# Ten of twelve down products by Strassen's scheme, in a recurrent layer followed by an MLP

## The chip, the cores and the metric

The kernel runs on one core of a Trainium2 chip. The metric is the time of one execution on the device in microseconds. A core has five engines that work from queues of their own, each in order: TensorE (PE in the profile, its weight loads PEld), VectorE (DVE), ScalarE (ACT), GpSimd (POOL) and SyncE (SP), which here issues the DMAs.

## The reference

Everything is float32. A recurrent block with a state of 40 x 40 for each of 4 x 8 heads runs over 768 steps; its output, 3072 tokens of 320 numbers, goes through a two-layer MLP.

```python
# r, k, v, w, a, b: (4, 8, 768, 40)
for t in range(S):
    y[:, :, t] = einsum('bhd,bhde->bhe', rt, state)
    Sa = einsum('bhde,bhe->bhd', state, at)
    state = state * wt[:, :, None, :] - einsum('bhd,bhe->bhde', Sa, bt)
    state = state + einsum('bhd,bhe->bhde', vt, kt)
x = y.transpose(0, 2, 1, 3).reshape(3072, 320)
h = x @ w_in                              # w_in: 320 x 2048
g = h * (1.0 / (1.0 + exp(-1.702 * h)))
return g @ w_out                          # w_out: 2048 x 320
```

## The kernel before, in words

The sequence is cut into 12 chunks of 64 steps. A *unit* i = 2c + p is chunk c for one pair p of the four batches, so there are 24 units. For each unit the kernel forms decays (`decay`), scores (`prep`), inverts a triangular matrix in five levels (`inverse`, PSUM tile `ps_level`, SBUF tiles W, E, ES, EX, T), and solves and updates the state (`solve`, tiles A, B, M, zr). The result x of a unit is written to DRAM and read back transposed as `xT` (`part_with`, `get_back`). When both units of a chunk are there, `mlp(c)` handles its 256 tokens.

All matmuls go through `mm` (line 300 of the profile) as 64 x 64 quarters of the array: `QUARTERS` walks over two halves r of the contraction and two halves of the output, so four matmuls of one step use four quarters. One such float32 matmul appears as two records in the profile.

`mlp(c)` has four steps q of the up product (`up`, tile `ps_up`, 256 columns, the tokens), each followed by an activation on ACT (`gelu`), which writes the tile g of q: 512 of the 2048 hidden numbers for the 256 tokens. The down product (`down(p)`, tile `ps_down`) takes 128 tokens at a time: eight parts m of two f of four quarters, 320 columns each, over the whole contraction. Then one engine copies one half of the PSUM pair to `ob`, VectorE adds the other, and SP stores `ob` with two DMAs. Four buffers of g are in turn.

The order of the work is written out by hand in the string `ORDER`: each entry names a task by its number, its engine by a letter (p, a, d, g, s for PE, ACT, DVE, POOL, SP) and the PSUM pair of the four that it uses. `Plan.add` registers a task with the engines that may do it and what it reads and writes; `Plan.listed` gives every task the engine and pair of its entry, and the tasks are issued in that order. So every engine's queue is the subsequence of the string with its letter. The costs that stand beside the tasks (`pe`, `dve`, `act`, `any2`) are not read when the kernel is built.

The weights come as 64-bit pieces (`weight`, raw data in the tile `extra` and in places that are free for the moment) and are made into float32 by ACT, VectorE and POOL in the first part of the run. `w_out_sb` holds w_out as 16 blocks f of 320 columns.

Of the kernel before, what the change touches and what calls it, by code (L numbers as in the profile page):

```python
# [58 lines left out]
class Plan:  # L59
# [29 lines left out]
    def listed(self, text):  # L89

        assert len(text.split()) == len(self.tasks)
        table, out, done = "exp", [], set()
        for one in text.split():
            e = next(e for e in ENGINES if ENGINES[e] in one)
            n, bank = one.split(ENGINES[e])
            t = self.tasks[int(n)]
            assert e in t.engines and t.after <= done and (e == "SP" or (t.pair is None) == (not bank))
            t.engine, t.bank = e, int(bank or 0)
            if e == "ACT" and t.table:
# [8 lines left out]
0s 8s 26s 5s 7s 9s 3a 6s 87p0 88p1 24s 89a1 1s 2s 12s 102a 95d 100p2 90a0 93d 158a 101d2 98p3 96g 10s 94d 17s 97g 16s 99d3  # L108
103p1 4a 11s 132p0 104a1 105d1 142p2 143p3 133a0 106d 130p1 14s 144a3 13s 107p0 15s 18s 151g 108a0 109d0 51s 131a1 110p3 27s
149g 150d 111a3 112d3 159p0 156p1 145a2 161d0 160a0 152g 113p3 345s 92a 162d 25s 153d 114a3 163p2 42s 115d3 34s 19a 274s 264p0  # L110
165d2 265p3 164a2 22d 266a3 166p2 20d 273s 21d 33s 43s 167a2 154p3 168d2 23g 35s 28a 157d1 116p2 155d3 169p1 117a2 118d2 267a0
279d 63s 280g 119p3 277s 171d1 36s 44s 123a3 120d3 343s 125d3 121a 278g 124d3 29d 287a 126p2 170a1 288p0 127a2 30d 172p1 479s
122a3 31d 289a0 128p2 54s 173a1 45s 129d2 32g 62s 174d1 134p3 37a 290d0 175p2 344s 135d3 180a2 146s 178a2 275s 176d2 136p1
179a2 38d 181a2 39d 177a 282g 276s 291d 91s 138a1 182p0 188p3 281d 183a0 186p2 139d 137a1 283p0 187a2 184p1 189a3 40d 140s
292p2 46a 60s 284d0 41g 285p3 185d1 148a 286d3 190p0 293a2 294d2 334p1 335p3 357a 191d0 141s 268g 147s 336a3 315d 192p2 47d
337a1 348d 316p0 194a2 346s 295p3 349d 61s 317a0 195g 347s 358p1 296a3 297d3 360d1 318a0 298p3 271a 361d 319p0 338g 300d3 196s
193a2 320a0 355p2 385d 270s 48d 299a3 362p0 356d2 351g 301p3 363a0 364d0 350g 386p2 197s 302d3 365p0 387a2 269s 352g 359a1
303d3 388a2 323p1 367d0 366a0 321p3 49d 324a1 304p2 322a3 478s 325d1 50g 353p0 309a2 470p3 354d0 209p1 307a2 210p1 310a2 305d2
211p1 308a2 272d 198p0 341a 199p0 72s 212p1 70s 64a 200p0 340s 368p2 52s 342d 339s 69s 201p0 369a2 202p0 370d2 203p0 471a
213p1 65d 214p1 389p2 66d 472a3 483g 204p0 390a2 560s 371p3 67d 306a 53s 215p1 71s 482s 216p1 372a3 217p1 476a 220p2 373d3 68g  # L120
218p1 221p2 477d 219a1 205p0 222p2 206p0 223p2 224p2 78s 559s 207p0 55a 311p3 225p2 79s 312d3 80s 226p2 208a0 58d 313p1 374p3
314d1 227p2 56d 379a3 228p2 229p2 57d 326p0 230a2 59g 393p1 327d0 378a3 391p2 394a1 375d3 231p0 558s 392d2 376a 232p0 233p0
395d1 81s 73a 234p0 480s 381p2 235p0 474s 328p1 475s 382a2 74d 377a3 485d 380a3 236p0 75d 481s 492a 242p2 486d 243p2 82a 76d
484d 77g 383p3 237p0 384d3 244p2 329d1 330d1 488p3 473d 238p0 531d 245p2 487g 246p2 489d3 85d 532p1 708s 239p0 533a1 396p3
331d 534a1 240p0 247p2 397d3 332s 241a0 562s 535p1 83d 490p3 536a1 84d 398p0 706s 572a 491d3 86g 550p1 253p3 399d0 551a 555s
400d0 561s 333s 254p3 401d 255p3 552a1 564d 493p0 402s 556a 567g 570p1 554s 494d0 248p2 705s 563d 566g 249p2 495d0 498d 256p3
571d1 565g 403s 250a2 496a0 251d2 696p1 497g 557d 539p0 252s 537p2 257p3 538a2 704s 540d0 701s 258p3 553d 611d 697a 499d 573p2
259p3 576a2 574d2 784s 710d 700s 260p3 787s 541d0 575d2 404p0 578d 261a3 577g 405p0 579d 698a1 568p2 711g 500p1 406p0 569d2
501a1 407p0 262d3 580p2 702a 502d1 263s 408p0 582d2 409p0 503d 410p0 583d 504a 612p3 411p0 584g 613d3 412p0 614d3 413p0 505p1
709d 414a0 426p3 506d1 427p3 428p3 507d1 429p3 699d 581d2 430p3 615p1 703d 431p3 616a1 785s 585p0 432p3 508d 586a0 433p3 587d0  # L130
434p3 509a 588d 435p3 589d 448p2 436a3 510p1 590p0 511a1 449p2 592d0 591a0 512d1 415p3 513d 416p3 593d 514a 417p3 594g 418p3
515p0 419p3 516a0 517d0 595p1 518d 420p3 596a1 597d1 421p3 598d 422p3 519a 599d 423p3 424p3 520p0 425a3 437p1 521d0 438p1
523d0 522g 439p1 524d0 440p1 525d0 441p1 442p1 526d0 527p3 718p0 528a3 443p1 719d0 929s 444p1 720d0 529p3 445p1 721d0 446p1
530d3 600p0 723d 447a1 542p3 722d 724g 603d0 605a0 619p1 604d0 543d3 450p2 620a1 606d0 544p3 621d1 601d0 602d 617p1 707s 546d3
451p2 618a1 783s 712d 547g 713d 607p0 725p1 608a0 452p2 609p0 453p2 548s 610d0 932s 454p2 727d1 726d1 622p0 728d 545d3 729a
775p1 455p2 623d0 780s 776a 549s 756d 730p3 624p0 456d2 457d2 731d3 458s 459p2 777a1 778g 732d3 786s 788g 781a 779s 626d0
460p2 625d0 627g 733d 795p1 835d 734a 461p2 735p3 791g 462p2 628s 736a3 796d1 737d3 716p0 792g 738d 463p2 782d 739g 1011s
920p1 757p3 925s 464p2 717d0 758a3 629s 759a3 790d 465p2 740p0 789d 466p2 741a0 742d0 921a 797p3 467d2 760p0 1008s 468d2 800a3
923d 652p2 469s 761d0 922a1 653p2 926a 930s 798d3 714p1 799d3 654p2 924s 802d 801g 655p2 934d 803a 656p2 836p0 657p2 715d1
658p2 659p2 837d0 762p3 838d0 927d 660p2 763a3 661p2 764p1 662a2 743d 630p0 744d 928s 631p0 632p0 765d1 804p3 766d1 633p0  # L140
805a3 806d3 634p0 807d 635p0 808a 745p2 636p0 748d2 637p0 749d2 839p1 933g 750d2 638p0 840a1 1009s 751d2 639p0 809p3 746d2
935g 640a0 641p1 810d3 642p1 793p2 747a 811d3 674p0 812d 794d2 813a 752p3 643p1 753a3 814p2 644p1 815a2 816d2 754p3 645p1
755d3 646p1 817d 647p1 818a 767p2 841p3 768d2 648p1 842a3 649p1 819p2 650p1 820a2 821d2 769p3 822d 651a1 823d 675p0 771d3 931s
770d3 772g 824p2 936d 676p0 827a2 828a2 942p1 829a2 677p0 1153s 830a2 937d 945a1 773s 663p3 825d2 664p3 943d1 1156s 826a 665p3
944d1 999p2 947d 946g 666p3 1000a 1004s 980d 940p1 948g 667p3 941d1 668p3 774s 669p3 670p3 831p1 671p3 1001a2 1002d 1003s
832d1 672p3 1005a 1013d 678p0 673a3 1006d 833p2 843p1 679p0 834d2 1007s 844d1 938p2 845d1 680p0 939d2 846p3 681p0 847d3 949p1
1012g 682d0 848p2 950a1 683d0 1014d 684s 685p3 849d2 1015g 1010s 850d2 1021p0 1016g 951d1 686p3 1024a0 1232s 851d 1235s 981p2
687p3 982a2 952d 852s 1022d0 983a2 953g 1144p1 1023d0 688p3 1026d 1145a 1149s 1025d 1027g 984p2 1059d 689p3 1154s 954p0 853s
985a2 1147g 690p3 1158d 1148s 955a0 956d0 986p2 1146a1 957d 1150a 691p3 958d 987a2 1151d 988p0 692p3 989a0 1152s 990d0 959p1
693a3 865p2 960a1 694d3 866p2 961d1 867p2 695s 962d 868p2 963d 1028p0 869p2 1029a0 1030d0 870p2 1031d 1157g 871p2 1159d 1032a  # L150
1060p3 872p2 873p2 1061a3 874p2 1062d3 1033p1 875a2 854p0 1035d1 855p0 1036d 856p0 1037d 1063p3 857p0 1064d3 1034a1 858p0
964p2 859p0 965a2 966d2 1038p1 967d 860p0 1039a1 1040d1 861p0 1041d 1017p3 968a 1042g 862p0 1018d3 863p0 969p2 864a0 876p1
970d2 877p1 972d2 971g 1043p3 973d2 878p1 1044a3 974d2 879p1 975d2 880p1 881p1 1045d3 1019p0 1046d 976p2 1047a 882p1 1020d0
1233s 883p1 977a2 1166p3 884p1 1169a3 1167d3 1377s 978p0 885p1 1168d3 898p2 1171d 1170g 886a1 979d0 887p3 1172a 1048p0 991p1
1051a0 888p3 1052a0 992d1 889p3 1053a0 890p3 1054a0 891p3 1049d0 993p1 1050a 1067p0 994d1 1160g 1155s 892p3 1161d 1068a0 893p3
894p3 1069d0 1380s 895p3 1204d 1065p0 995d1 896p3 996d 1066a0 1231s 1055p1 899p2 897a3 1056d1 997s 1173p0 1223p3 900p2 1174a0
# [92 lines left out]
def rwkv7_gelu_quick(ctx: ExitStack, tc: tile.TileContext, time_d, v_d, w_d, wc_d, ak_d, b_d, rv_d, w_in, w_out, out):  # L249
    nc = tc.nc  # L250
    H, D, S = 8, 40, out.shape[0] // 4
    DM = H * D
    C = 64
    MID = C // 2
    NU = time_d.shape[0]
    PIECE = w_in.shape[2]
    NF = w_in.shape[0] * PIECE // DM
# [717 lines left out]
    def mlp(c):  # L975
# [47 lines left out]
        for p in BITS:  # L1023
            down(p)
# [8 lines left out]
    for i in range(NU):  # L1033
# [10 lines left out]
        if i % 2:  # L1044
            mlp(i // 2)
# [84 lines left out]
```

## Time and profile before

| | |
|---|---|
| median of three runs | 679.92 us (675.03 to 681.91) |
| profiled execution | 682.79 us |
| its span, first to last instruction | 681.1 us |
| granted TensorE clock, mean | 0.990 |
| PE busy | 652.0 us, 96% of the span |
| DVE, ACT, POOL busy | 445.5, 330.7, 176.7 us |
| busy time of the group ps_up | 254.4 us, 3840 records |
| busy time of the group ps_down | 240.3 us, 3072 records |
| the chain that ended last | PE 91%, DMA 4% |

In a group's line of the profile come the source line, engine and operation, the tiles, the shapes, the number of records, then busy time and the mean length of one. Records of matmuls overlap each other: the 3072 of ps_down last 430 ns each on the mean, but one starts every 70 ns or so. In the slices the span is cut into 40 parts of 17 us, with the busy share of each in tenths. The timeline merges neighbouring instructions of one kind into one line: start, length from the first start to the last end, and how many.

### The profile page before, as it was taken

Reading aid. Unit: us, or ns where it says so; the run is one execution under the profiler, and the core shown is the slowest. Engines: PE = TensorE matmul, PEld = TensorE weight load, DVE = VectorE, ACT = ScalarE, POOL = GpSimd, SP = SyncE. Lnnn points to the kernel's source line nnn. Section 1 sums busy time; section 2 is a strip of 40 time slices with the busy share of each in tenths; the row PEclk is TensorE's granted clock in tenths of the full one; section 3 lists DMA queues with packets and bytes.
Section 4 is the critical chain, followed back from the end, with each engine's and each line's share of the span. In section 5 each row is a group of like instructions: output and inputs, shape, how many; then the busy total and the mean of one; then the engine's idle time right before and its main releaser. Section 6 shows DMA issues by size and latency. Waiting matters only on the chain.

```text
span 681.1 us, 42181 instructions
## 1 busy us (share of the span) xinstructions
PE 652.0 (96%) x19488; PEld 572.4 (84%) x19488; DVE 445.5 (65%) x906; ACT 330.7 (49%) x688; POOL 176.7 (26%) x204
## 2 busy tenths in 40 slices
PE   5777999999999999999999999999999999999997
PEld 5667888997987788888888898899899799889996
DVE  4687877777867668767776587868556766675001
ACT  4675845544564654664545445455454354252110
POOL 5443444225123123123123211321412421300000
PEclk9788999999999999999999999999999999999999
DMA  7874755205314314432404413513502312200100
GB/s 235 275 244 148 228 158 173 89 14 155 108 50 139 103 45 125 124 108 67 121 23 131 140 34 107 154 33 106 149 29 71 121 51 58 58 13 23 51 12 21
DMA packets 35312, 69.73 MB, mean 102 GB/s; under 512 B 5440, under 2 KB 14656, under 8 KB 35136
## 3 DMA queue, kind: packets, MB, share of 16 engines
q1 hardware_dynamic: 35136, 67.03, 32.8%
q8 instruction: 153, 2.51, 1.6%
q14 instruction: 23, 0.19, 0.1%
HBM read 59.15 MB, written 7.86 MB: 98 GB/s over the span
## 4 chain that ended last, share of the span: by engine, by line
PE 91%; DMA 4%; ACT 1%; DVE 1%; issue 1%; SPq 0%; ACTq 0%; DVEq 0%
PE ps_up L300 31%; PE ps_down L300 30%; PE ps_level L300 9%; PE ps_y L300 5%; PE ps_B L300 4%; PE ps_X L300 2%; PE ps_N L300 2%; PE ps_rz L300 2%; PE ps_RV L300 2%; PE ps_A L300 1%; DMA ak<-in_ak 1%; PE ps_zT L300 1%; PE ps_Q L300 1%; DMA time<-in_time 1%; PE ps_T L300 1%
## 5 line engine op out<-in xcount | busy, mean ns | idle before, releaser
L300 PE MATMUL ps_up<-xT_all,w_sb 64*64 64x256 f32 x3840 | 254.4, 377 | 2.0 <-DMA xT_all<-x_dram 1.1
L300 PE MATMUL ps_down<-w_sb,g 64*64 64x320 f32 x3072 | 240.3, 430 | 1.1 <-issue 0.9
L300 PEld LDWEIGHTS ps_up<-xT_all,w_sb 64*64 64x64 f32 x3840 | 172.9, 133 | 17.7 <-issue 2.5
L300 PEld LDWEIGHTS ps_down<-w_sb,g 64*64 64x64 f32 x3072 | 143.3, 133 | 31.4 <-issue 1.6
L988 ACT ACTIVATE g<-ps_up 128x1024 f32<-128x1024 f32 x48 | 49.1, 1024 | 44.7 <-PE ps_up L300 44.3
L709 POOL TENSOR_TENSOR EX<-ES,quads 128x512 f32<-128x512 f32 x29 | 38.3, 1323 | 115.5 <-DVE ES L702 83.1
L751 ACT COPY W<-ps_level 128x512 f32<-128x512 f32 x56 | 32.7, 585 | 69.1 <-PE ps_level L300 67.4
L300 PEld LDWEIGHTS ps_level<-W,EX 64*64 64x64 f32 x2560 | 59.2, 134 | 5.8 <-DVE T L830 0.2
L300 PE MATMUL ps_level<-W,EX 64*64 64x64 f32 (+1 forms) x2560 | 56.2, 217 | 0.0
L753 DVE TENSOR_TENSOR E<-two,ps_level 128x256 f32<-128x256 f32 x80 | 33.1, 415 | 34.7 <-ACT W L751 30.7
L707 ACT ACTIVATE EX<-ES,quads 128x256 f32<-128x256 f32 x80 | 36.3, 501 | 30.4 <-DVE ES L702 29.9
L619 POOL TENSOR_TENSOR ak<-ak,FT 128x512 f32<-128x512 f32 x16 | 22.0, 1378 | 76.2 <-DMA ak<-in_ak 54.4
L300 PE MATMUL ps_level<-PT,EX 64*64 64x64 f32 (+2 forms) x1280 | 34.9, 244 | 5.7 <-DVE EX L723 4.8
L300 PEld LDWEIGHTS ps_level<-PT,EX 64*64 64x64 f32 x1280 | 32.6, 145 | 8.9 <-DVE EX L723 5.7
L702 DVE STREAM_TRANSPOSE ES<-E 128x256 f32<-128x256 f32 x80 | 35.2, 442 | 4.7 <-DVE E L753 0.5
L300 PE MATMUL ps_y<-M,bh 64*64 64x104 f32 (+1 forms) x768 | 34.8, 247 | 1.3 <-DVE M L907 0.8
L300 PE MATMUL ps_y<-RV,kh 64*64 64x104 f32 (+1 forms) x768 | 34.9, 247 | 0.3 <-DVE EX L723 0.3
L891 ACT COPY B<-ps_B 128x416 f32<-128x416 f32 (+1 forms) x34 | 16.5, 492 | 33.5 <-PE ps_B L300 33.2
L300 PEld LDWEIGHTS ps_y<-RV,kh 64*64 64x64 f32 x768 | 28.9, 133 | 2.0 <-DVE M L907 0.5
L907 DVE TENSOR_TENSOR M<-ps_X,later 128x832 f32<-128x832 f32 (+1 forms) x24 | 23.8, 993 | 9.8 <-PE ps_X L300 9.5
L627 POOL TENSOR_TENSOR kh<-time,G 128x320 f32<-128x320 f32 x18 | 16.2, 902 | 48.4 <-PE ps_y L300 34.4
L300 PEld LDWEIGHTS ps_y<-M,bh 64*64 64x64 f32 x768 | 27.0, 133 | 1.9 <-DVE M L907 1.2
(131 smaller groups left out, 1097.2 us busy)
## 6 DMA issues: line engine op xcount, KB each, us to landing
ak<-in_ak SPq DMA_DIRECT2D x48, 160.0 KB
rv<-in_rv SPq DMA_DIRECT2D x48, 160.0 KB
time<-in_time SPq DMA_DIRECT2D x24, 320.0 KB
xT_all<-x_dram SPq DMA_DIRECT2D x48, 160.0 KB
wc<-in_wc SPq DMA_DIRECT2D x20, 264.0 KB
logw<-in_w SPq DMA_DIRECT2D x24, 160.0 KB
RV<-in_v SPq DMA_DIRECT2D x24, 160.0 KB
b<-in_b SPq DMA_DIRECT2D x48, 80.0 KB
```

The source lines that it names most:

```text
L300: nc.tensor.matmul(o, lhsT, rhs, start=start, stop=True, skip_group_check=True)
L619: plan.add(R, {"DVE": 690.0, "POOL": 1270.0, "sbuf": True}, lambda t: of(t.engine).tensor_mul(ahT(), ahT(), FT_of(i)), reads=T("ak", "FT") ...
L627: plan.add(R + 4, {"POOL": 870.0, "DVE": 490.0, "sbuf": True}, lambda t, n=n, dst=dst: of(t.engine).tensor_mul(dst(i)[:, :, :D], by_head(t ...
L702: plan.add(rank, dve(256), lambda t: nc.vector.transpose(ES(n), source(t)), writes=[key("ES", n, 6)], **reads)
L707: nc.scalar.activation(dst[:, :, h], ES(n), ACT.Copy, scale=quads[:, h, :1])
L709: of(t.engine).tensor_mul(dst, ES(n).unsqueeze(2).to_broadcast([128, 8, 2, 32]), quads.unsqueeze(1).to_broadcast([128, 8, 2, 32]))
L751: plan.add(rank, any2(512), lambda t: copy(t.engine)(tiles_of(W(n + 1)), blocks(psum(t, ""), 64)), writes=[key("W", n + 1, 5)], pair=pair)
L753: plan.add(rank, dve(256), lambda t: nc.vector.tensor_sub(tiles_of(E(n + 1)), every(two32, [128, 2, 4, 32]), blocks(psum(t, ""), 64)[:, :, ...
L891: plan.add(R, any2(4 * wide), lambda t: copy(t.engine)(dst(), some(psum(t, "")[:, :, :208])), writes=[("Bv", i)] if x and c > 0 else T("B" ...
L907: plan.add(R + 1, dve(8 * wide), lambda t: nc.vector.tensor_tensor(M_of(i)[:, :, :wide].rearrange("p (j b) n -> p b j n", b=2), some(psum( ...
L988: plan.add(-45, {"ACT": 1030.0, "table": "gelu"}, lambda t: nc.scalar.activation(g_of(c * NQ + q).rearrange("p m r n -> p r m n"), psum(t, ...
```

## The change

For chunks 2 to 11 (`FAST`) the down product is computed by Strassen's scheme (in the form with seven products and fifteen additions). The 256 tokens are split into two halves p, the contraction of 2048 into two halves s, the 320 output columns into two halves d of 160. Seven products of 128 x 1024 by 1024 x 160 take the place of eight. The four differences of blocks of w_out that the scheme needs, T1 to T4, are formed once (`factors`) in `extra`, after the weights are ready. For each fast chunk, four combinations of blocks of g (S1 to S4) are formed, three of them in place in g, each in two parts j; the products go to three PSUM pairs (`ps_fast`, with two, three and two products); and their sums form the four blocks of the output in `of_fast`, with `new6` and `new7` between. The last chunk computes the product M2 last, and stores in three steps, the last of them half on ACT's queue.

The layout of g changes for all chunks, so that one half of the tokens is contiguous; there are six buffers of g and not four. The string `ORDER` is new as a whole, 2840 entries in place of 2700. A scratch area that the program reserves is set to 2048 bytes; no DMA here is issued by POOL. The other two chunks keep the old form of the down product.

```diff
+    FAST = range(2, 12)
...
-                     ... xT=3, g=4, ob=1), 4)
+                     ... xT=3, g=6, ob=1, S10=1, S11=1, of=1, n6=1, n7=1), 4)
...
-    g_of = lambda n: buf("g", n, [128, 2, 2, 256])
+    g_of = lambda n: buf("g", n, [128, 2, 4, 128])
+    DH = DM // 2
+    S1 = single("S1", [128, 2, 4, 128])
+    T1, T2, T3, T4 = (extra[:, k * PIECE:(k + 1) * PIECE].rearrange("p (j f n) -> p j f n", j=2, f=4) for k in range(4))
+    B11, B12, B21, B22 = (w_out_sb.rearrange("p (j s f d n)": ...)[:, :, s, :, d] for s in BITS for d in BITS)
+    of_fast, new6, new7 = (single(name, [128, n, DH]) for name, n in (("of_fast", 4), ("new6", 3), ("new7", 2)))
+
+    def factors():
+        for dst, a, b, ... in ((T1, B12, B11), (T2, B22, T1), (T3, B22, B12), (T4, B21, T2)):
+            for j in BITS:
+                ... of(t.engine).tensor_sub(dst[:, j], a[:, j], b[:, j])
+
+    def fast_down(c):
+        last = c == NU // 2 - 1
+        def mixed(j, name, dst, a, b, reads, writes, add=False):      # POOL or DVE, 128x512
+            ... (of(t.engine).tensor_add if add else of(t.engine).tensor_sub)(dst(j), a(j), b(j))
+        def product_of(pair, n, at, a, b, j, reads, first=True):
+            def go(t):
+                po = psum(t, "ps_fast")
+                for f in range(4):
+                    for r, h in QUARTERS:
+                        mm(po[HALF[h], r, at * DH:(at + 1) * DH], a(j)[HALF[r], 2 * (f % 2) + f // 2, h * 64:h * 64 + 64], b[HALF[r], j, f],
+                           first and at == 0 and j == 0 and f == 0)
+        def summed(pair, n, dst, key, name, free=()):                 # ACT or DVE copies, DVE adds
+            ... copy(t.engine)(flat(), psum(t, "")[:, 0, :n * DH])
+            ... nc.vector.tensor_add(flat(), flat(), psum(t, "")[:, 1, :n * DH])
+        def added(dst, a, b, n, reads, uses, name):                   # POOL or DVE, n * 160 columns
+            ... of(t.engine).tensor_add(dst(), a(), b())
+
+        for j in BITS:
+            mixed(j, "A", s1, A21, A22, ..., add=True)                # S1
+            mixed(j, "S3", A21, A11, A21, ...)
+        if last:
+            products(0, *((1, 0, M1, j) for j in BITS))
+        else:
+            products(0, *((n, n % 2, M, j) for j in BITS for n, M in ((2, M2), (1, M1))))
+        S4 = s1 if last else A12
+        for j in BITS:
+            mixed(j, "S2", A11, s1, A11, ...)
+            if not last:
+                mixed(j, "S4", S4, A12, A11, ...)
+        if not last:
+            summed(0, 2, lambda: of_fast[:, :2], "of", "M21")
+            added(of_fast[:, 0], of_fast[:, 0], of_fast[:, 1], 1, ..., "C11")
+        else:
+            summed(0, 1, lambda: of_fast[:, 1:2], "of", "M21")
+        products(1, *((4, 0, M4, j) for j in BITS), *((5, 1, M5, j) for j in BITS), *((6, 2, M6, j) for j in BITS))
+        if last:
+            for j in BITS:
+                mixed(j, "S4", S4, A12, A11, ...)
+        summed(1, 3, lambda: new6, "n6", "M456")
+        added(new6[:, 2], new6[:, 2], of_fast[:, 1], 1, ..., "U")
+        added(new6[:, :2], new6[:, :2], new6[:, 2] broadcast, 2, ..., "XW")
+        products(2, *((n, at, M, j) for j in BITS for n, at, M in ((7, 0, M7), (3, 1, M3))))
+        summed(2, 2, lambda: new7, "n7", "M73")
+        added(of_fast[:, 1], new6[:, 1], new7[:, 1], 1, ..., "C12")
+        added(of_fast[:, 2:], new6[:, :2], new7[:, 0] broadcast, 2, ..., "C2")
+        if last:
+            store(0, ["C12"], slice(1, 2))
+            store(1, ["C2"])
+            ... M2 in pair 0, summed into of_fast[:, 0:1] ...
+            store(0, ["C11"], slice(0, 1))                            # second DMA on ACT's queue
+        else:
+            store(0, ["C11", "C12"])
+            store(1, ["C2"])
...
-        for p in BITS:
-            down(p)
+        if c in FAST:
+            fast_down(c)
+        else:
+            for p in BITS:
+                down(p)
...
+            if i // 2 == min(FAST):
+                factors()
             mlp(i // 2)
...
-    nc = bacc.Bacc("TRN2", target_bir_lowering=False, num_devices=1)
+    nc = bacc.Bacc("TRN2", target_bir_lowering=False, num_devices=1, dynamic_dma_scratch_size=2048)
```

In the fast products, M1 is A11 by B11, M2 is A12 by B21, M3 is S4 by B22, M4 is A22 by T4, M5 is S1 by T1, M6 is S2 by T2 and M7 is S3 by T3, where A are blocks of g and B blocks of w_out.

More of the change, by code (lines that the diff above doesn't have):

```diff
@@ L98, in listed @@
             t.engine, t.bank = e, int(bank or 0)
+            if e == "SP":
+                t.window = t.bank
             if e == "ACT" and t.table:
@@ L245 @@
+2607d 2806d 2609s 2815p1 2810d 2816p1 2819d 2817p1 2820d 2818p1 2811d0 2825p3 2821d1 2822d1 2826p3 2812d0 2823d 2827p3 2824d
+2828p3 2835p0 2829d3 2830d3 2836p0 2831d 2832d 2833s 2834s 2837d0 2838d0 2839s
 """
```

340 lines of the change are left out of this document (198 added, 142 removed).

## The prediction

> **What bounds the kernel now.** I read the page first: its engine table and its slices.
>
> ```profile
> span 681.1 us, 42181 instructions
> ...
> PE 652.0 (96%) x19488; PEld 572.4 (84%) x19488; DVE 445.5 (65%) x906; ACT 330.7 (49%) x688; POOL 176.7 (26%) x204
> ...
> PE   5777999999999999999999999999999999999997
> ...
> DVE  4687877777867668767776587868556766675001
> ...
> PEclk9788999999999999999999999999999999999999
> ```
>
> From the fifth slice (68 us) on TensorE is full, at a full granted clock; VectorE comes next with some seven tenths. The part that is not full is the opening. The sums by stretch say the same in microseconds (columns: length, then busy time of PE, weight loads, DVE, ACT, POOL, then granted clock, DMA share, GB/s):
>
> ```profile
> 0.00:100.00 100.00, 77.76 (x2478) 69.45 (x2482) 70.37 (x109) 62.68 (x148) 46.04 (x66) 0.93 0.70 216
> ...
> 300.00:400.00 100.00, 100.00 (x3062) 85.85 (x3054) 71.66 (x154) 50.38 (x90) 24.63 (x28) 1.00 0.34 96
> ```
>
> 22 us of the 29 us that PE is idle lie in the first 100 us. The waits of TensorE name only small ones: 4.8 us for EX, 3.8 us for the first logw, 1.1 us once for x coming back by DMA. So outside the opening a matmul taken out of the order shortens the span by its own streaming time, as long as what feeds it keeps up.
>
> Busy means are no price here, since spans of neighbouring groups overlap. The timeline of a full stretch gives prices by the distance between starts:
>
> ```profile
> 413.88 0.49 PE L300 MATMUL ps_cum<-logw,edges 64*64 64x160 f32 x6
> 414.16 1.28 PE L300 MATMUL ps_down<-w_sb,g 64*64 64x320 f32 x16
> ...
> 417.01 0.57 PE L300 MATMUL ps_B<-RV,A 64*64 64x104 f32 x16
> 417.37 0.57 PE L300 MATMUL ps_B<-zr,ak 40*64 40x104 f32 x16
> 417.73 1.28 PE L300 MATMUL ps_down<-w_sb,g 64*64 64x320 f32 x16
> 418.81 0.67 PE L300 MATMUL ps_A<-ak 40*64 40x64 f32 x32
> ```
>
> From 417.73 to 418.81 sixteen matmuls of 320 columns start and give way: 67.5 ns each. From 417.37 to 417.73 sixteen of 104 columns: 22.5 ns. The end of the chain agrees and adds the third point:
>
> ```profile
> 657.91 4.32 PE ps_up L300 x80
> 662.23 14.02 PE ps_down L300 x208
> ```
>
> 14.02 us / 208 = 67.4 ns at 320 columns, 4.32 us / 80 = 54.0 ns at 256. Through 22.5, 54.0 and 67.4 runs nearly one straight line of 0.21 ns a column with less than 1 ns beside it.
>
> **TensorE's part.** The group of the down product has 3072 matmul records, 256 for each of 12 chunks. Ten chunks lose theirs: 2560 x 67.4 ns = 172.5 us go. Each of the ten gets seven products of two halves j, four f and four quarters, two records each: 7 x 64 = 448 records of 160 columns, 4480 in all. No long run of 160 columns is in the trace. Between 104 and 256 columns the line gives 22.5 + 56 x 0.207 = 34.1 ns; the lower end is half of 67.4, 33.7 ns; the upper is the short ps_cum burst, whose eight records lie between 413.84 and 414.16, 40 ns each, with the last ps_zT among them. I take 34.1, from the long runs. 4480 x 34.1 ns = 152.8 us come, so **-19.7 us** (-21.5 at 33.7; +6.7 at 40).
>
> [...]
>
> **What feeds it.** Each fast chunk needs eight additions of 128x512 out of SBUF, three reads of PSUM in two steps, and five additions of their sums. By the written order VectorE gets 49 of the 512-wide ones and POOL 31. Nearest rows for VectorE, 128x512: 699 ns (EX by quads), 740 ns (ak by GT), 924 ns (ak by FT). I take 0.72 us: 49 x 0.72 = 35.3 us. Reads of PSUM on VectorE, 45: from the rows at 320 columns (483 and 489 ns) and estimates of 0.33 and 0.65 us at 160 and 480, 23.5 us. Sums, 35: 19 x 0.33 + 16 x 0.50 = 14.3 us. Six of the eight weight differences at 0.85 (estimate): 5.1 us. Away go 24 - 4 additions and nine copies of ob, 14 us. VectorE goes from 445.5 to about 510 us, some 77% of the new span. ACT gains 17 PSUM copies and loses 11; POOL gains 31 x 1.38 us (its row for ak by FT) and about 14 smaller, and stays under 40%. None of them is a bound over the whole.
>
> What counts is cover at each place. Walking down the order with the prices above, no Strassen product reads an operand whose last addition is listed less PE work ahead than that addition lasts; so I cost these waits at nothing. If the cover goes, a product waits for one addition, 0.7 us. The cover is thinner than before: after the first 100 us of PE work 114 of PE's steps have less than 0.5 us to spare beyond their latest feeder; in the old order it was 30. With those the old kernel left PE idle for 2 us between 100 and 600 us of the span. I charge **+2 us** (0 to +8). The thinnest stretch stands from 475 to 550 us of PE work: 74.6 us of TensorE beside about 69 us of VectorE (52 us in the old order).
>
> Also in this account is the way of x through DRAM to the next up product. The old order has 7.8 to 11.5 us of PE work there after the first chunk, and the chunk with 9.8 waited 1.1 us for DMA. Three chunks now have 7.3 to 7.6, six have more than before.
>
> The two store steps of a fast chunk issue two DMAs each on SP, as the two stores did; at the last chunk there are three steps, the third split between SP and ACT, where ACT has nothing left.
>
> **Opening and tail.** The first 75 PE lines come in nearly the same order. But until 62 us of PE work VectorE carries more: three ak products come from POOL, four PT copies of 768 from ACT (918 ns each on VectorE), about 9 us in all, against a busy 70 of 100 us. I take +1 us (-3 to +6). At the end the last copy and addition shrink from 320 to 160 columns, 0.98 to about 0.66 us, and the last store is half as large and issued from two queues: -0.5 us. The 448 records after the last up are covered by the products of chunk 10 that stand among them.
>
> **Sum.** The profiled execution took 682.79 us, 1.7 around its span of 681.1. 681.1 - 19.7 + 2 + 1 - 0.5 = 663.9 of span, 665.6 as a run. That execution stands 2.9 us over the median of 679.92, so in terms of the median **663 us**, -2.5%. About 1% is what a measurement of this kernel can tell from no change (its three runs lie from 675.03 to 681.91).
>
> **Rivals.**
> - *VectorE becomes the bound.* For: the 924 ns row, were it the rule, adds 49 x 0.2 = 10 us, and the thin stretch then holds 71 to 72 us of VectorE against 74.6, with an in-order queue on either side. Against: in the slices where VectorE shows eight tenths PE still shows nine or more. Half of that 10 us and three more lost in the opening give 668 to 677. [...]
> - *Slower: short matmuls do not stream.* In every one of the 140 product bursts the weight load (133 ns mean) has to hide behind 4 x 34 = 136 ns of the same quarter, against 270 before. Break-even is 172.5 / 4480 = 38.5 ns a record; at the 40 ns of the ps_cum burst, 682.79 + 6.7 + 2.5 - 2.9 = 689 us. Against: at 104 columns the load has 90 ns and the run still goes at 22.5. [...]
> - *Instructions run short, so the change brings little.* 3840 more instructions for TensorE, 15 more packets of 256. The instruction queue's 153 packets took 1.6% of 16 engines' span, 1.1 us each; if each new one stops PE for that long, +17 us, 680. Against: waits of PE for "issue" come to 3.5 us in all, and all lie before 100 us.
> - *Better:* no thin cover bites and the opening gains its 3 us: under 657.
>
> **Chances.** Forecast (657 to 668) 0.62; better 0.09; VectorE 0.17; instructions 0.07; slower by short matmuls 0.05. The range to the ends of the VectorE case leaves out the last two and half of the better one: 654 to 677. Faster by over 1% (under 673.1) takes the first two and 0.13 of the third: 0.84; within 1%: 0.04 + 0.07 = 0.11; slower 0.05.
>
> **What would show it.** Right: a group ps_fast with 4480 records whose starts lie 33.5 to 34.5 ns apart, PE still nine tenths or more in every slice from the fifth on, VectorE near 510 us busy. Wrong: ps_fast at 38 ns or more; PE waits on S, g or n6 by VectorE or POOL of more than a few us in total; waits for xT_all; a first stretch of 100 us with less than 75 us of PE; "issue" waits behind 100 us.

## The result, and the profile after

The changed kernel takes 706.13 us (median of four runs, 705.17 to 715.19) against 680.1 us beside it (675.03 to 681.91): the ratio is 1.043, with an interval from 1.035 to 1.051. It is slower. The forecast was 663 us, with a range of 654 to 677. The profiled execution is the longest of the four, with a span of 713.5 us; the other three had spans of 703.4 to 705.2 us. So where sizes matter the text also uses a second profiled execution of the same kernel (`after_again` below, span 696.0 us). The ratios in the table below leave out executions more than 1.5% above the fastest of their kernel, which concerns `a_lean` alone: three of its ten, 690.79 to 693.40 us, while its median is that of all ten.

The page of after: first the engine table, the slices and the instruction queue, then the chain's first line and two groups.

```profile
span 713.5 us, 46101 instructions
...
PE 657.4 (92%) x21408; PEld 589.8 (83%) x21408; DVE 498.0 (70%) x1001; ACT 347.0 (49%) x737; POOL 201.4 (28%) x227
...
PE   5766889999998999999899999999999899999997
...
DVE  6677967868777777667776777867766778875515
...
PEclk9869999999999999999999999999999999999999
...
q8 instruction: 168, 2.75, 1.6%
...
PE 82%; DVE 7%; issue 5%; DMA 3%; SPq 1%; ACT 1%; POOL 1%; POOLq 0%; DVEq 0%; ACTq 0%
...
L310 PE MATMUL ps_fast<-extra,g 64*64 64x160 f32 x1920 | 82.5, 297 | 4.7 <-issue 4.3
L310 PE MATMUL ps_fast<-w_sb,g 64*64 64x160 f32 x1856 | 77.1, 297 | 0.6 <-issue 0.6
```

TensorE's busy time rose from 652.0 to 657.4 us although its streaming shrank; records of matmuls last several times their distance (the two groups above: 297 ns on the mean, with a start every 33.9 ns) and reach into short pauses, so busy time is no measure of the work here. The slices show more: from the fifth on they were all at nine but the last, and now five of them are at eight. VectorE is at seven tenths and is not the bound. The chain's share of "issue", time in which an engine waits for nothing that the profile shows, went from 1% to 5%. The instruction queue brings 168 packets in place of 153. TensorE's 21,408 matmuls and 21,408 weight loads, divided by 168, are 255 a packet; before, 38,976 / 153 = 255. With the 264 semaphore and drain instructions that the trace has of this queue it is 43,080 / 168 = 256.4. So a packet (2.75 MB / 168 = 16.4 KB) is 256 instructions, and in effect all of these packets are TensorE's.

The sums by stretch (columns as before) give the place: each stretch between 100 and 700 us lost 2 to 8 us of PE, where before they were full to about 1 us. The clock is not the reason: it was granted in full (1.00) in these stretches but one (0.98).

```profile
0.00:100.00 100.00, 74.06 (x2317) 66.50 (x2321) 73.90 (x116) 55.92 (x136) 34.97 (x58) 0.90 0.64 201
...
200.00:300.00 100.00, 92.82 (x3175) 86.22 (x3171) 72.70 (x148) 56.39 (x117) 34.50 (x32) 1.00 0.30 87
300.00:400.00 100.00, 96.48 (x3298) 86.11 (x3294) 68.47 (x143) 52.77 (x104) 39.56 (x48) 1.00 0.32 94
400.00:500.00 100.00, 98.13 (x3340) 91.59 (x3334) 73.76 (x148) 53.90 (x116) 41.78 (x43) 1.00 0.31 90
500.00:600.00 100.00, 92.11 (x3156) 82.39 (x3151) 70.69 (x154) 45.11 (x98) 17.42 (x18) 0.98 0.27 79
```

And this is what TensorE waited for behind 100 us (columns: us in total, times, longest):

```profile
PE ps_fast L310 <- issue: 5.7, 9, 1.1
PE ps_B L310 <- issue: 3.9, 4, 2.3
PE ps_up L310 <- issue: 3.4, 8, 1.1
PE ps_level L310 <- issue: 3.0, 5, 1.7
```

All of the larger ones end in "issue", and not only at the new products: the old steps (ps_B, ps_up, ps_level) stop as well. Over this stretch the waits for "issue" add up to 22.7 us, 35 times (before: 0.5 us, once); everything else that TensorE waited for there adds up to 1.6 us (before: 1.5). No wait for S or new6 is among them.

The timeline shows where in the instruction stream such a stop falls. In brackets stands the idle time ahead of a line.

```profile
204.31 0.37 PE L310 MATMUL ps_y<-RV,kh 64*64 64x104 f32 x8
204.49 0.35 PE L310 MATMUL ps_y<-M,bh 64*64 64x104 f32 x7
206.32 0.30 PE L310 MATMUL ps_y<-M,bh 64*64 64x104 f32 x1 [1.48 <-issue]
206.32 1.59 PE L310 MATMUL ps_up<-xT_all,w_sb 64*64 64x256 f32 x24
...
214.32 0.27 PE L310 MATMUL ps_A<-ak 40*64 40x64 f32 x2 [0.23 <-issue]
...
215.04 1.36 PE L310 MATMUL ps_fast<-w_sb,g 64*64 64x160 f32 x32
216.13 0.92 PE L310 MATMUL ps_X<-B,T 64*64 64x104 f32 x31
...
217.27 0.63 PE L310 MATMUL ps_level<-PT,EX 64*64 64x64 f32 x28
219.63 0.27 PE L310 MATMUL ps_level<-PT,EX 64*64 64x64 f32 x2 [1.73 <-issue]
```

From 204.49 on seven of eight ps_y matmuls start; the eighth, of the same step with the same operands, comes at 206.32. No operand can be late there: its neighbours read the same tiles. From 206.32 up to the small stop at 214.32 the trace has 254 matmuls, 254 weight loads and 4 semaphore instructions of this queue, 512 in all; from there up to 219.63 it has 127, 128 and 1, which is 256. So two packets lie between the first two stops and one between the next two. In the trace, packets of the instruction queue begin at 203.41, 207.52, 211.99 and 217.27 us, and TensorE starts again at 206.32, 214.32 and 219.63. So TensorE stops where a packet ends, and starts some 2.3 to 2.9 us after the next one began to come.

This holds for the whole run. If all instructions of this queue are counted in the order of their starts, a packet ends at the 193rd instruction of the trace and at every 256th behind it. Of the 35 waits for "issue" behind 100 us, 34 lie within eight places of such an end (22.4 us of them). The same count gives 278 of the 281 waits of all thirteen profiles of this document. Places so near to an end are 7% of all places.

The lines at 215.04 and 216.13 carry another reading: 32 fast matmuls in 1.09 us, 34.1 ns each. Over all undisturbed runs of 16 the median is 33.9.

### The profile page after: what moved, and what is told of

Read it like the earlier page. It is cut to its first block, busy times and chain, and to the rows that moved or that the text cites. A ratio compares the mean times of both kernels' runs of the same rounds, so it can differ in the third digit from the quotient of the medians.

```text
span 713.5 us, 46101 instructions
## 1 busy us (share of the span) xinstructions
PE 657.4 (92%) x21408; PEld 589.8 (83%) x21408; DVE 498.0 (70%) x1001; ACT 347.0 (49%) x737; POOL 201.4 (28%) x227
## 3 DMA queue, kind: packets, MB, share of 16 engines
q8 instruction: 168, 2.75, 1.6%
## 4 chain that ended last, share of the span: by engine, by line
PE 82%; DVE 7%; issue 5%; DMA 3%; SPq 1%; ACT 1%; POOL 1%; POOLq 0%; DVEq 0%; ACTq 0%
PE ps_up L310 28%; PE ps_fast L310 20%; PE ps_level L310 9%; PE ps_B L310 5%; PE ps_y L310 4%; PE ps_down L310 4%; PE ps_X L310 3%; PE ps_N L310 2%; PE ps_A L310 2%; PE ps_RV L310 1%; PE ps_rz L310 1%; DVE x L963 1%; DMA ak<-in_ak 1%; PE ps_zT L310 1%; PE ps_cum L310 1%
## 5 line engine op out<-in xcount | busy, mean ns | idle before, releaser
L310 PEld LDWEIGHTS ps_up<-xT_all,w_sb 64*64 64x64 f32 x3840 | 164.8, 134 | 35.1 <-issue 12.3
L310 PE MATMUL ps_fast<-extra,g 64*64 64x160 f32 x1920 | 82.5, 297 | 4.7 <-issue 4.3
L310 PE MATMUL ps_fast<-w_sb,g 64*64 64x160 f32 x1856 | 77.1, 297 | 0.6 <-issue 0.6
L310 PEld LDWEIGHTS ps_fast<-extra,g 64*64 64x64 f32 x1920 | 70.0, 133 | 6.8 <-issue 6.8
L1112 ACT ACTIVATE g<-ps_up 128x1024 f32<-128x1024 f32 x48 | 49.2, 1024 | 52.5 <-PE ps_up L310 48.6
L310 PEld LDWEIGHTS ps_fast<-w_sb,g 64*64 64x64 f32 x1856 | 67.6, 133 | 1.7 <-issue 1.2
L717 ACT ACTIVATE EX<-ES,quads 128x256 f32<-128x256 f32 x114 | 51.4, 501 | 24.3 <-DVE ES L712 23.9
L310 PEld LDWEIGHTS ps_level<-PT,EX 64*64 64x64 f32 x1280 | 34.1, 149 | 12.9 <-issue 7.9
L807 ACT COPY Tc<-ps_level 32x64 f32<-32x64 f32 x120 | 24.3, 203 | 32.2 <-PE ps_level L310 18.7
L310 PE MATMUL ps_down<-w_sb,g 64*64 64x320 f32 x512 | 39.4, 429 | 0.0
L310 PE MATMUL ps_B<-RV,A 64*64 64x104 f32 (+1 forms) x768 | 31.6, 257 | 2.4 <-DVE EX L733 1.4
L917 DVE TENSOR_TENSOR M<-ps_X,later 128x832 f32<-128x832 f32 (+1 forms) x24 | 23.8, 994 | 13.7 <-PE ps_X L310 13.5
L310 PE MATMUL ps_B<-zr,ak 40*64 40x104 f32 (+1 forms) x704 | 28.6, 247 | 3.9 <-issue 3.9
```

Of the source, the lines that this page charges most:

```text
L310: nc.tensor.matmul(o, lhsT, rhs, start=start, stop=True, skip_group_check=True)
L717: nc.scalar.activation(dst[:, :, h], ES(n), ACT.Copy, scale=quads[:, h, :1])
L807: copy(t.engine)(dst, src[:, u, :, f])
L917: plan.add(R + 1, dve(8 * wide), lambda t: nc.vector.tensor_tensor(M_of(i)[:, :, :wide].rearrange("p (j b) n -> p b j n", b=2), some(psum( ...
L1112: plan.add(-45, {"ACT": 1030.0, "table": "gelu"}, lambda t: nc.scalar.activation(g_of(c * NQ + q).rearrange("p q b n -> p b q n"), psum(t, ...
```

## The experiments

Two theories of the author's at the start. **Instruction supply**: a packet of 256 instructions needs a certain time from the moment TensorE enters the one before it (estimated at 3.3 to 4 us from the distances of packets: behind 100 us two of them begin at least 3.27 us apart in the trace of after, 3.34 in that of before); where its 128 matmuls stream faster than that, TensorE stops at the end of a packet. **Thin covers**: operands of the products come late, because VectorE or POOL has too much to do, and the profile puts the wait down to the wrong thing. A third reading is that short matmuls cost something each.

To measure the loss in all runs alike, the time between 100 us and 15 us before the end was taken, less the sum of the prices of the matmul records that start in it (33.9 ns at 160 columns, 53.9 at 256, 67.4 at 320, about 22 at 104, 14.6 at 64, 135.8 for a whole-array matmul of 160). This is called the *steady loss*. Its zero depends on the prices of the shortest forms (for before 2 to 8 us come out), but the differences between runs change by 2 us at most. "At ends" is the part of it, to about 1 us, that lies within eight places of the end of a packet, by the count above. The last column is the sum of TensorE's waits for "issue" behind 100 us; it is smaller, since the modelled end of the last matmul reaches into each stop (the wait at 206.32 above reads 1.48 us, where the start before it lies 1.73 us back).

| run | time, us | ratio to before (95%) | TensorE records | packets | steady loss, us | at ends, us | "issue", us |
|---|---|---|---|---|---|---|---|
| before | 680.1 | 1 | 19,488 | 153 | 2.0 | 2 | 0.5 |
| after | 706.13 | 1.043 (1.035 to 1.051) | 21,408 | 168 | 49.4 | 37 | 22.7 |
| after_again | 698.44 | 1.031 (1.028 to 1.035) | 21,408 | 168 | 34.8 | 21 | 14.8 |
| b_split | 716.21 | 1.056 (1.053 to 1.058) | 22,048 | 173 | 39.5 | 29 | 16.7 |
| b_split_q | 729.38 | 1.070 (1.066 to 1.074) | 22,048 | 173 | 48.4 | 42 | 28.8 |
| b_split_5 | 711.32 | 1.045 (1.042 to 1.048) | 20,768 | 163 | 31.8 | 28 | 19.2 |
| b_quarter_5 | 764.86 | 1.127 (1.120 to 1.134) | 23,328 | 183 | 89.9 | 77 | 65.8 |
| a_nomix | 696.01 | 1.029 (1.024 to 1.034) | 21,408 | 168 | 34.3 | 25 | 12.6 |
| a_wide | 701.07 | 1.035 (1.031 to 1.039) | 18,048 | 142 | 36.6 | 8 | 3.6 |
| a_lean | 686.97 | 1.003 (0.999 to 1.007) | 19,168 | 150 | 24.3 | 17 | 11.6 |
| a_lean_nomix | 678.29 | 0.999 (0.996 to 1.002) | 19,168 | 151 | 13.5 | 9 | 5.1 |
| tail2 | 679.34 | 0.998 (0.9949 to 1.0005) | 19,872 | 156 | 5.4 | 5 | 1.7 |
| tail2_wide | 675.05 | 0.996 (0.993 to 0.999) | 19,200 | 151 | 2.3 | 1 | 0.4 |

### The changed kernel again

No edit.

> The changed kernel once more, for a second profile and times beside the others. Instruction supply (my theory now: each packet of 256 instructions for TensorE needs some 3.3 to 4 us from the moment the one before it is begun, and the 1920 additional short matmuls bring the packets nearer than that): 168 packets again, PE gaps of 0.5 to 2 us again just ahead of packets, 703 to 716 us. Thin covers (the rival: products wait for additions on VectorE and POOL): the same time, but waits of ps_fast on S, g or n6 should make up most of what PE loses.

698.44 us (697.77 to 702.41) beside 677.69, below the 703 to 716 that were expected. The stops are there again, fewer: 22 waits for "issue" behind 100 us, 21 of them at packet ends, and no product waits for S, g or n6. The median time moved too: the ratio was 1.043 in the first series of runs and is 1.031 in this one, so two series of one kernel can lie over 1% apart. The size of the effect differs between executions by some 15 us of steady loss; its kind does not.

### The old kernel with its down matmuls cut in two

The edit, written in the form of the next runs:

```diff
-    for r, b in QUARTERS:
-        mm(po[HALF[b], r, :DM], ..., w_out_sb[HALF[r], f * DM:(f + 1) * DM], f == 0)
+    wide = 160 if 2 <= c < 12 else DM
+    for r, b in QUARTERS:
+        for h in range(0, DM, wide):
+            mm(po[HALF[b], r, h:h + wide], ..., w_out_sb[HALF[r], f * DM + h:f * DM + h + wide], f == 0 and h == 0)
```

> The kernel before, with each 320-column matmul of the down product of chunks 2 to 11 issued as two of 160 columns. Same order, same columns, same additions; 2560 more matmul records, 5120 more instructions, 20 more packets. Instruction supply: slower by 15 to 45 us (from the spacing of packets that the order gives, with 3.5 to 3.8 us for a packet), so 695 to 725 us, with the gaps ahead of packets. Thin covers: no change, 677 to 683 us, as nothing has been added on any other engine.

716.21 us, 5.6% over before. Nothing was changed on VectorE, POOL or ACT, no addition came in, the order is the old one. This edit alone slows the old kernel down by more than the whole change did. One doubt was left: the two halves of a matmul follow each other on the same quarter of the array. The next run has the loops the other way round, so that neighbours are on different quarters:

```diff
+    for h in range(0, DM, wide):
+        for r, b in QUARTERS:
+            mm(...)
```

> As b_split, the kernel before with two matmuls of 160 columns for each of 320 in chunks 2 to 11, but with the four quarters of the first half issued ahead of the four of the second, so that no quarter takes two matmuls one after the other. Instruction supply alone: 695 to 715 us. If b_split was slow because neighbouring matmuls shared a quarter: back at 680 to 690 us.

729.38 us: slower still, so the same quarter was not the reason. The estimate was too low. Whether this order of the halves is itself worse than the other isn't shown: the two were run on different chips, and their ratios (1.070 and 1.056) lie hardly further apart than the two series of the changed kernel.

28 of the waits for "issue" are at the cut matmuls, and old steps have some too:

```profile
PE ps_down L300 <- issue: 20.0, 28, 1.7
PE ps_B L300 <- issue: 3.4, 4, 1.3
```

### Cut in two in five chunks only

`2 <= c < 7` in place of `2 <= c < 12`.

> As b_split_q, but in chunks 2 to 6 alone: 1280 more matmul records, 10 more packets. Instruction supply: about half the loss of b_split_q, 686 to 700 us, with the stalls in the first half of the run (100 to 400 us) and none new behind it.

711.32 us. The estimate was again too low, but the place is as the theory has it. In the sums by stretch PE is short only while chunks 2 to 6 run, and full again behind 500 us:

```profile
100.00:200.00 100.00, 99.24 (x3128) 85.79 (x3122) 73.85 (x157) 51.50 (x107) 29.15 (x31) 1.00 0.34 100
200.00:300.00 100.00, 90.10 (x3101) 84.04 (x3096) 63.25 (x128) 47.96 (x104) 22.80 (x21) 1.00 0.32 92
300.00:400.00 100.00, 94.17 (x3208) 88.61 (x3199) 65.22 (x137) 49.06 (x86) 23.87 (x28) 1.00 0.31 86
400.00:500.00 100.00, 96.45 (x3249) 91.63 (x3253) 67.50 (x146) 44.84 (x95) 19.35 (x20) 1.00 0.29 86
500.00:600.00 100.00, 99.73 (x3046) 87.39 (x3042) 66.58 (x137) 46.57 (x102) 26.97 (x31) 1.00 0.27 79
```

### Cut in four in the same five chunks

`wide = 80` in place of 160. TensorE's work stays nearly the same; the number of its instructions in these stretches grows so far (128 matmuls of 17.2 ns are 2.2 us) that by the first theory the supply must be the bound.

> The kernel before with the 320-column matmuls of the down product cut into four of 80 columns, in chunks 2 to 6 alone: 1280 records become 5120, nothing changes on the other engines. By streaming it changes little (80 columns on the line through 22.5, 54.0 and 67.4 ns are about 17 ns, so some 2 us more). TensorE then wants 256 instructions (128 matmul records and 128 weight loads) every 2.2 us. Theory (instruction supply): in these stretches the packets of the instruction queue start at one steady distance, and TensorE's time is that distance times the packets. Walking the order with one price a packet gives +72 us at 3.4 us a packet, +92 at 3.65, +127 at 4.0: 755 to 810 us in all. Rival (a fixed cost of each short matmul, 19 to 24 ns by the two halved kernels): +73 to +92 us, but then with idle time spread over the matmuls and not at the packets' places.

764.86 us (two runs), within the 755 to 810 of the supply theory. The rival, a fixed cost of each short matmul, had +73 to +92 us and so nearly the same time; what tells them apart is where the idle time lies. Where 80-column matmuls run without a stop they take 17.2 to 17.3 ns each (60 of them from 305.04 to 306.08 below), as the straight line through the longer ones says, so there is no fixed cost of a short matmul. The timeline of one stretch:

```profile
304.79 0.39 PE L300 MATMUL ps_level<-W,EX 64*64 64x64 f32 x11 [1.45 <-issue]
304.97 0.28 PE L300 MATMUL ps_down<-w_sb,g 64*64 64x80 f32 x3
305.02 0.22 PE L300 MATMUL ps_level<-W,EX 64*64 64x64 f32 x1
305.04 1.25 PE L300 MATMUL ps_down<-w_sb,g 64*64 64x80 f32 x60
306.08 0.23 PE L300 MATMUL ps_RV<-rv 40*64 40x64 f32 x2
306.12 0.23 PE L300 MATMUL ps_down<-w_sb,g 64*64 64x80 f32 x1
306.13 0.63 PE L300 MATMUL ps_RV<-rv 40*64 40x64 f32 x29
306.55 0.28 PE L300 MATMUL ps_down<-w_sb,g 64*64 64x80 f32 x3
306.60 0.22 PE L300 MATMUL ps_RV<-rv 40*64 40x64 f32 x1
306.62 0.51 PE L300 MATMUL ps_down<-w_sb,g 64*64 64x80 f32 x17
308.17 0.98 PE L300 MATMUL ps_down<-w_sb,g 64*64 64x80 f32 x42 [1.04 <-issue]
...
311.64 0.42 PE L300 MATMUL ps_down<-w_sb,g 64*64 64x80 f32 x10 [1.11 <-issue]
```

From 304.79 up to the stop, 11 + 3 + 1 + 60 + 2 + 1 + 29 + 3 + 1 + 17 = 128 matmuls start, exactly one packet with their loads; then TensorE stands for 1.04 us, and the next 128 begin at 308.17. The starts after a stop lie 308.17 - 304.79 = 3.38 and 311.64 - 308.17 = 3.47 us apart: this is the time that a packet takes when TensorE waits for nothing else. In the trace packets begin at 305.92 and 309.31 us, 1.13 and 1.14 us after TensorE entered the packet before; TensorE goes on 2.25 and 2.33 us after they began. Behind the opening, no two of these packets began less than 3.2 us apart in any of the thirteen profiles. The idle time sits at the ends of packets and not between matmuls (all 55 waits for "issue" behind 100 us, and some 77 of the 90 us of steady loss), which is what tells the supply from a cost for each matmul.

### The changed kernel without the additions S1 to S4

```diff
-    (of(t.engine).tensor_add if add else of(t.engine).tensor_sub)(dst(j), a(j), b(j))
+    pass
-    s1 = lambda j: S1[:, j]
+    s1 = lambda j: A21(j)
```

> The changed kernel without the combinations S1 to S4 of the blocks of g: the 80 additions of 128x512 are left out, and the products read blocks of g as they are (S1 is replaced by A21), so the output is not the product. TensorE's instructions and their order are the same. Instruction supply: little change, 695 to 710 us. Thin covers: VectorE loses 35 us and POOL 43 us and no product waits for them, so 660 to 675 us.

696.01 us against 698.44 for the whole change on the same chip; the intervals of the ratios overlap (1.024 to 1.034 and 1.028 to 1.035), the steady loss is 34.3 against 34.8. Eighty additions on VectorE and POOL, with all their waits and their memory traffic, are worth 2 us or nothing. The covers of these additions are not the cause of the loss.

### The products in whole-array matmuls

One 128 x 128 matmul in place of four quarters: a quarter of the products' instructions, the same work.

```diff
-    for r, h in QUARTERS:
-        mm(po[HALF[h], r, at * DH:(at + 1) * DH], a(j)[HALF[r], 2 * (f % 2) + f // 2, h * 64:h * 64 + 64], b[HALF[r], j, f], ...)
+    mm(po[:, f % 2, at * DH:(at + 1) * DH], a(j)[:, 2 * (f % 2) + f // 2, :], b[:, j, f], ...)
```

> The changed kernel with each group of four quarter matmuls (64x64) of the fast products issued as one matmul of 128x128, two of the four f into each of the two PSUM banks, so that all that follows stays as it is. 1120 records of ps_fast in place of 4480, 142 packets in place of 168. Instruction supply: the spacing of packets that the order gives leaves about half of the loss, 680 to 695 us, if a wide matmul of 160 columns takes the 134 ns of four quarter ones; if wide weight loads are not hidden, ps_fast's records will lie further apart than 134 ns and the time rises by 1120 times the difference. Thin covers: no gain, 700 to 710 us.

701.07 us, no gain in time: the 680 to 695 of the supply theory did not come, and the time alone would fit the other theory. But the waits changed their kind: "issue" falls from 14.8 to 3.6 us, and the loss at packet ends from 21 to 8 us. A whole-array record takes 135.8 ns, four times the quarter's 33.9. The largest part of the loss is now at the 147 places where TensorE goes from 128 x 128 to 64 x 64 or back: 18.9 of the 34.6 us above before, some 0.13 us each. So the fewer instructions did what the theory says, and the switches gave most of it back; some 10 us of this run's loss have no place in this account.

### The products with half the instructions, in quarters

The matmuls take 320 columns over two f; half of the contraction is left out, so the amount of streaming stays.

```diff
-    for f in range(4):
+    o = min(at * DH, 192)
+    for f in (0, 2):
         for r, h in QUARTERS:
-            mm(po[HALF[h], r, at * DH:(at + 1) * DH], ..., b[HALF[r], j, f], ...)
+            mm(po[HALF[h], r, o:o + 2 * DH], ..., b[HALF[r], j, f:f + 2], ...)
```

> The changed kernel with each fast product issued in matmuls of 320 columns over two of the four f in place of 160 over four: half the contraction is left out and columns are written that nobody asked for, so the output is not the product. Columns streamed, order, additions and waits are those of the changed kernel; ps_fast has 2240 records in place of 4480, and TensorE about 150 packets of instructions in place of 168. Instruction supply: nearly all that TensorE lost between 100 us and the end comes back (from the spacing of packets, 5 us left in place of 35), 658 to 672 us. Anything else that the changed kernel has (its additions, its order, the way of x): no gain, 693 to 703 us.

686.97 us, ratio 1.003 (0.999 to 1.007). With the order, the additions and the streaming unchanged, most of the loss against before is gone, but the gain of the scheme does not show: 24 us of steady loss are left, 17 of them at packet ends. The 658 to 672 expected did not come. Two things could hold the rest: dense stretches of short matmuls in the new order itself, or covers, which would matter only once the supply no longer hides them. So the same without the additions:

```diff
     # a_lean, and
-    (of(t.engine).tensor_add if add else of(t.engine).tensor_sub)(dst(j), a(j), b(j))
+    pass
```

> The lean kernel (fast products in 320-column matmuls over two f, half of their contraction left out) with the additions S1 to S4 taken away as well. If thin covers hold up the lean kernel's 24 us of steady loss, 10 us or more come back: under 677 us. If it is the order's stretches of short matmuls outside the products (instruction supply), as with the additions' removal from the changed kernel itself (-2.4 us): 0 to -4 us, 683 to 687.

678.29 us, ratio 0.999 (0.996 to 1.002). In the two profiles the steady loss falls from 24.3 to 13.5 us, but the intervals of the two ratios overlap, and the medians were taken on different chips. The time is neither the under 677 of the covers nor the 683 to 687 of the supply. The places say more: of the 10.8 us by which the loss falls, some 8 lie at packet ends, so the stops in a_lean are for the most part those of the supply. Why they shrink without the additions is not settled. Its largest waits behind 100 us are still "issue":

```profile
PE ps_up L310 <- issue: 1.7, 5, 0.6
PE ps_level L310 <- issue: 1.6, 2, 1.0
```

### The scheme in the last two chunks only

At the end of the run there are fewer short matmuls beside the products. `FAST = range(10, 12)`, with the old order up to the last up products of chunk 10 and a new end behind them.

> Strassen's scheme in chunks 10 and 11 alone, in the order of the kernel before, with a new end: their products stand where hardly any of the short matmuls of the recurrence are left. 2 x (256 x 67.4 - 448 x 33.94 ns) = 4.1 us less to stream and a tail shorter by 0.3 us. Instruction supply: 128 pairs of 160 columns take 4.3 us, so packets stay far enough apart and the gain stands: 672 to 676 us where the kernel before takes 678. If the fast products lose time by themselves wherever they stand: 678 us or more.

679.34 us, ratio 0.998 (0.9949 to 1.0005), beside 681.06 for before on this chip. The 4 us of streaming that two chunks save did not come out as a gain that can be told from none; 3.4 us more of steady loss than before stand against it, about 3 of them at packet ends. With the whole-array matmuls of a_wide in these two chunks:

> Strassen's scheme in chunks 10 and 11 alone, each fast product in 128x128 matmuls in place of four quarters: a quarter of the instructions of the products. The run with quarters took 679.34 with 4.3 us of gaps at packets; these should go (-3 to -4 us), and some 25 to 30 switches between 128x128 and 64x64 at 0.13 us come (+3 to +4): 677 to 681. A version clearly under the kernel before (below 674) needs the switches to be fewer than that.

675.05 us, ratio 0.996 (0.993 to 0.999). That is better than the 677 to 681 expected. "issue" is back at 0.4 us, and there are only eleven switches of the mode (1.5 us) in place of the 25 to 30 expected, because the products stand together. The interval lies just below 1, so this version is ahead of the kernel before, on the chip where both ran (679.21), by some 0.4% (0.1 to 0.7), and clearly ahead of the changed one.

## Why the prediction was wrong, point by point

**The step that failed is the one that was not in the sum.** The working charged TensorE for streaming, for feeding, for the opening and for the tail, and let 1920 more matmuls and as many loads cost nothing as instructions. In its place the runs showed 33 to 47 us: the steady loss of after_again and after, less the 2.0 us of before, some 19 to 35 us of it in stops at packet ends. The old kernel slowed down in the same way (39.5 us of steady loss) when only its matmuls were cut in two.

**The rival "instructions run short" named the thing, but priced it wrongly.** It took 15 additional packets at 1.1 us, the time a packet spends on the DMA queue, got 680 us and gave it a chance of 0.07. As the runs read, the price is not paid for additional packets but for each packet whose 128 matmuls stream in less than the distance of two packets, 3.38 and 3.47 us where b_quarter_5 waits for nothing else. By the prices of the trace, 128 matmuls of 320 columns last 8.6 us, of 160 columns 4.3, of 104 columns 2.9, of 64 columns 1.9. By this the fast products alone would not stop (4.3 against 3.4 us). But between them stand the short matmuls of the recurrent part, and a packet that is half of those and half of 160-column ones lasts 3.1 us, where it lasted 5.2 with 320 columns. The long down matmuls had paid for the short ones. A walk along the written order with one time for every packet gives the steady losses with about 3.4 us a packet in before, 3.6 in b_quarter_5, 3.7 to 3.9 in the two executions of after, 3.75 to 3.85 in the three kernels cut in two. One time does not fit all; the distance is set at 3.4 us or so by what b_quarter_5 shows when nothing else waits, and why it is longer elsewhere is open.

**The argument against that rival was a misreading.** The 3.5 us of waits for "issue" are right. That they all lie before 100 us is not: one of the six stands at 197 us.

```profile
PE ps_y L300 <- issue: 0.5, 1, 0.5
```

And all six lie at the ends of packets, by the count above: the old kernel ran short already, now and then. The sum of these waits is small, but it does not say how near to the limit the kernel stood everywhere else. The mean was in the page: 153 packets over some 627 us of TensorE's streaming are one every 4.1 us; the 168 of the new one over 606.4 us are one every 3.6. The time a packet needs could not be read from the trace of before with certainty, but its shortest distance behind the opening, 3.34 us, was there.

**The price of a 160-column record was right**: 34.1 ns forecast, 33.9 measured over undisturbed runs, so 4480 x 33.9 - 172.5 = -20.6 us against -19.7. The rival "short matmuls do not stream" is refuted by it, and by 17.2 ns at 80 columns. Of the 346 bursts of 16 in the two executions, 18 took more than 36 ns a record, and 16 of these have the end of a packet in them.

**Feeding was sized about right as far as the change as it is goes.** TensorE waited 1.6 us behind 100 us for anything but instructions (3.0 in after_again, 1.5 before), and the run without the additions shows no measurable gain; +2 had been charged, 0 to +8. What the covers would cost if the supply were cured is the open point of a_lean_nomix. The additions lasted about as estimated: 679, 733 and 703 ns in the rows below for 0.72 us, and the reads of 480 columns of PSUM 652 ns for 0.65 us. VectorE's total came to 498.0 us against about 510. It did not become the bound.

```profile
L1013 DVE TENSOR_TENSOR g<-g 128x512 f32<-128x512 f32 x23 | 15.6, 679 | 0.2
...
L1013 DVE TENSOR_TENSOR S<-g 128x512 f32<-128x512 f32 x13 | 9.5, 733 | 19.4 <-ACT g L1112 18.6 <-PE ps_fast L310 0.8
...
L1013 DVE TENSOR_TENSOR g<-S,g 128x512 f32<-128x512 f32 x13 | 9.1, 703 | 1.5 <-PE ps_fast L310 1.4
...
L1030 DVE TENSOR_TENSOR new<-new,ps_fast 128x480 f32<-128x480 f32 x10 | 6.5, 652 | 2.9 <-ACT new L1029 2.8
```

**The opening** took about 4 to 7 us more than before by the same account as the steady loss, for +1 (-3 to +6) forecast: PE has 74.06 us there in place of 77.76. That is under the 75 us which the prediction had named as a sign of being wrong. A wait of 4.0 us for T by VectorE at ps_X, 0.7 before, is the largest piece, and a wait for "issue" at ps_N another 2.3:

```profile
PE ps_X L310 <- DVE T L840: 4.0, 2, 3.3
...
PE ps_N L310 <- issue: 2.3, 1, 2.3
```

No experiment took the opening apart. The granted clock of these 100 us was 0.90 in after and 0.93 in after_again and before, which may be a part of the 3 us between the two executions.

**The sum with what was measured**: 681.1 - 20.6 (streaming) + 6.8 (opening) + 47.4 (steady loss) = 714.7, where the span is 713.5; for the second execution 681.1 - 20.6 + 3.9 + 32.8 = 697.2, span 696.0. The 1.2 us that are left are within what the prices allow.

## What to carry to other kernels

Price a change on TensorE in instructions as well as in columns: add up, along the written order, how long each 128 matmuls with their loads last, and compare it with the distance of two packets of 256 instructions (3.4 to 3.9 us by the walk above). A kernel can stand just above that limit with hardly a wait to show for it (3.5 us here, 0.5 of it behind the opening), and where such waits lie in the instruction stream tells more than their sum; an engine that is full at one instruction length is no proof that it can be fed at half the length (2.0 us of steady loss in before, 39.5 in b_split). Where work is to be cut into more, smaller matmuls, put them together and make each as large as the array allows (tail2_wide, with eleven switches of the mode: 0.996 of the time before; a_wide, with 147: 1.035), and keep the long ones next to the short ones (by the prices above a packet half of 64 columns lasts 5.2 us beside 320 columns, 3.1 beside 160).

## What the runs showed of the hardware that was not expected

- TensorE was bound by the supply of its instructions: behind the opening of no run did two packets of 256 begin less than 3.2 us apart, and where b_quarter_5 waited for nothing else, the starts after its stops lay 3.38 and 3.47 us apart. At a stop the next packet began 1.2 to 1.9 us after TensorE had entered the one before (median of the stops in each run), and was used 2.16 us after it began at the earliest, 2.4 to 2.6 us as a median, though its transfer lasts only about 1 us (median 1.03 us in after). At some stops it began much later (217.27 in the timeline of after, 2.95 us behind 214.32); what delays those isn't in the profile.
- Quarter-array matmuls in float32 stream at 0.21 ns a column without a fixed part down to 80 columns (17.2 ns; 33.9 at 160, 53.9 at 256, 67.4 at 320), as long as instructions are there.
- A switch between 128 x 128 and 64 x 64 matmuls costs some 0.13 us: 147 of them 18.9 us in a_wide, eleven of them 1.5 us in tail2_wide.
